# RetNet attention followed by a PReLU feed-forward on one core: the next block's first attention unit enters in the last visit of the block before

## The chip, the cores and the metric

The kernel runs on one core of a Trainium2 chip. The metric is device time in microseconds (us), the median of several executions. In the profile the engines are PE (TensorE, matrix products), PEld (its weight loads), DVE (VectorE), ACT (ScalarE), POOL (GpSimd) and SP (SyncE, which here issues nearly all the DMAs). PSUM is the memory into which the matrix products write; it has eight banks, each of 512 float32 columns on 128 partitions.

## The reference

Two stages follow each other. The first is a retention recurrence per batch and head, with a state of 64 × 64 that decays by a factor of the head; the second is a feed-forward layer over the 3072 tokens, with a leaky ReLU whose slope is learned per hidden column.

```python
batch, n_heads, seq, head_dim = (4, 8, 768, 64)
...
gamma = 1.0 - 2.0 ** (-5.0 - np.arange(H, dtype=np.float32))
scale = 1.0 / np.sqrt(D)
for t in range(S):
    state = gamma[None, :, None, None] * state + np.einsum('bhd,bhe->bhde', k[:, :, t], v[:, :, t])
    y[:, :, t] = scale * np.einsum('bhd,bhde->bhe', q[:, :, t], state)
...
n_tokens, d_model, d_ff = (3072, 512, 2048)
h = x @ w_in
g = np.maximum(h, 0.0) + alpha * np.minimum(h, 0.0)
return (g @ w_out).astype(np.float32)
```

## The kernel before

**Units.** The recurrence is worked in chunks. A unit is 256 positions of one batch and four heads; there are 24 of them, `w` = 0 to 23, two (the head groups) for each stretch of 256 positions. Within a unit the positions form two chunks of 128. Four units (`WB`) make one block of 512 tokens, and there are six blocks, `n` = 0 to 5. Units 4n to 4n + 3 yield the transposed activations `xT[n]` that block n's feed-forward takes.

**What a unit needs.** `load` fetches k, q and v on SP's queue, four units ahead. `prep` scales k and q by their decays on POOL and casts v; from unit 8 on a transposing DMA on SP turns the result into `kq`. `ahead()` does the next unit's `prep` and, behind it, the load of the unit four further on.

**What a unit does on PE, in steps.** All of it is in products on quarters of 64 × 64 of the array.
- `scores(w)` (line 260) multiplies k and q into a pair of PSUM banks with tag `s`; `state_sums(w)` (line 284) multiplies k and v into one or two banks with tag `p`.
- On DVE, `masked(w)` (line 295) turns the scores into the float16 tile `m2`, and so frees `s`; `state(w)` (lines 309 and 311) adds the carried state and decays it, and so frees `p`. A unit with two chunks that both carry on has four such steps.
- `within(w)` (line 344) multiplies the masked scores with v into a pair of banks with tag `y`, then makes the first part of the products with the carried state (line 322). A tiny DVE memset (line 357) behind them tells that they are through.
- `finish(w)` makes the second part of the carried products (line 322 again), which wait for that memset, and ACT copies `y` into `xT` (line 373).

`visit(w_old, w_new)` interleaves two neighbours: `within(w_old)`, `scores(w_new)`, `state_sums(w_new)`, `finish(w_old)`, then `masked(w_new)` and `state(w_new)`. Either may be `None`.

**The feed-forward of a block.** Both halves are generators; `tick(gen, m)` issues the next m matmuls, so that units can be put in between.
- `ffn1(n)` (line 427) makes 16 tiles of 512 hidden columns' worth of output, four matmuls each, 64 in all. For each tile ACT makes `hm` (line 407) and DVE the leaky ReLU (line 396, called a prelu here). Its tiles take their PSUM banks in a written order: `f` is one of two banks `fa` and `fb` in turn, `p` the pair of state banks, and `s`, `S`, `y`, `Y` the first and second halves of the pairs that the units also use.
- `ffn2(n)` (line 444) makes four output tiles of 128 tokens, 16 matmuls of 512 columns each, 64 in all, into `fa` and `fb` in turn. ACT copies each into `os` (line 453), and SP stores it (line 457).

**The order.** The program is scheduled by hand: each engine runs its instructions in the order of the calls, and waits only where data or a buffer asks for it. In the loop for n = 1 to 5, `ffn1(n)` runs with calls of `ahead()` in between, and `ffn2(n)` takes the units of block n + 1 in between: unit w0 = 4(n + 1) enters alone after 2 ticks, three joint visits follow 14 ticks apart, and unit w0 + 3 leaves alone, `within` after 12 more ticks and `finish` 2 ticks later. Six ticks are left. `ahead()` is called at tick 24 and at tick 50. The last block, n = 5, has no units to take in.

Of the kernel before, what the change touches and what calls it, by code (L numbers as in the profile page):

```python
# [9 lines left out]
FP = mybir.dt.float32  # L10
F16 = mybir.dt.float16
COPY = mybir.ActivationFunctionType.Copy
# [6 lines left out]
def kernel(  # L19
# [15 lines left out]
    nc = tc.nc  # L35
    B, H, S, D = q.shape
    d_model, d_ff = moe_w_in.shape
    NFT = d_ff // 128
# [3 lines left out]
    NW = 2 * B * NUS  # L42
    WB = 4
    NBLK = NW // WB
    TB = 512
    scale = 1.0 / np.sqrt(D)
# [31 lines left out]
    sbp = ctx.enter_context(tc.tile_pool(name="sbp", bufs=1, space=bass.MemoryType.SB))  # L78
# [14 lines left out]
    w_out_all = sbp.tile([128, NFT, d_model], F16, tag="wout", name="wout")  # L93
# [5 lines left out]
    def ps(name, tag, n=512, dt=FP, bufs=2):  # L99
        if tag == "f":  # L100
            tag = ("fa", "fb")[flip[0] % 2]
            flip[0] += 1
        if tag in ("fa", "fb"):
            bufs = 1
        return psp.tile([128, n], dt, tag=tag, bufs=bufs, name=name)
# [32 lines left out]
    def place(w):  # L138
        u, g = divmod(w, 2)
        b, c3 = divmod(u, NUS)  # L140
        return u, g, b, c3
# [106 lines left out]
    def half(i):  # L248
        return slice(64 * i, 64 * i + 64)
# [64 lines left out]
    def carried(w, y, started, same, after=None):  # L314
        u, g, b, c3 = place(w)
        kq = live[w][1]
        for x in range(2):
            for r in range(2):
                c = r if same else 1 - r
                if c3 + c == 0:  # L320
                    continue
                ins = nc.tensor.matmul(  # L322
                    out=y[half(x), 256 + 256 * c + 128 * r : 384 + 256 * c + 128 * r],
                    lhsT=tgs[2 * u + c, g][half(r), x, :],
                    rhs=kq[half(r), 4 + 2 * x : 6 + 2 * x, half(c)],
                    start=(c, x) not in started,
                    stop=(same == (c == r)),
                    skip_group_check=True,
                )
                started.add((c, x))  # L330
                if after is not None:
                    behind(ins, after, "the other row half wrote this bank")
                    after = None
        return ins

    def within(w, mid=None, teller=None):
        u, g, b, c3 = place(w)
        vx, m2 = live[w][2:4]
        y = ps("y", "y", 1024, FP, 1)
        started = set()  # L340
        for r in range(2):
            for a in range(2):
                for c, x in DIAG:
                    nc.tensor.matmul(  # L344
                        out=y[half(x), 256 + 256 * c + 128 * r : 384 + 256 * c + 128 * r],
                        lhsT=vx[half(c), 2 * r + x, a, :],
                        rhs=m2[half(c), 2 * r + x, a, :],
                        start=(c, x) not in started,
                        stop=(a == 1 and c3 + c == 0),
                        skip_group_check=True,  # L350
                    )
                    started.add((c, x))
        if mid:
            mid()
        last = carried(w, y, started, True)
        if teller != nc.scalar:
            done = (teller or nc.vector).memset((warm if teller is None else bell)[0:1], 0.0)  # L357
        else:
            done = teller.activation(
                out=word[0:1], in_=word[0:1], func=COPY, bias=0.0, scale=1.0  # L360
            )
        behind(done, last, "tells that the products within the chunks are through")
        live[w].append((y, started, done))

    def finish(w):
        u, g, b, c3 = place(w)
        y, started, done = live[w].pop()
        carried(w, y, started, False, done)
        live.pop(w)
        n, i = divmod(u, 2)  # L370
        if w % WB == 0:
            xT[n] = sbp.tile([128, 2, 4, 2, 128], F16, tag="xT", bufs=2, name=f"xT{n}")
        nc.scalar.activation(  # L373
            out=xT[n][:, g, 2 * i : 2 * i + 2].rearrange("p c r (i a) -> p (c r) i a", a=2),
            in_=y[:, 256:768].rearrange("p (s a i) -> p s i a", a=2, i=64),
            func=COPY,
            bias=0.0,
            scale=1.0,
        )

    def visit(w_old, w_new, cs=None):
        if w_old is not None:
            within(w_old)
        if w_new is not None:
            scores(w_new)
            state_sums(w_new, cs)
        if w_old is not None:
            finish(w_old)
        if w_new is not None:
            masked(w_new)  # L390
            state(w_new, cs)
# [13 lines left out]
    def minus(hps):  # L405
        hm = sbp.tile([128, TB], FP, tag="hm", bufs=3, name="hm")
        nc.scalar.activation(out=hm, in_=hps, func=RELU, bias=0.0, scale=-1.0)  # L407
        return hm

    def ffn1(n, order="spyfSpYf", lead=(0, 0)):  # L410


        gt = sbp.tile([128, NFT, TB], F16, tag="gt", bufs=2, name=f"gt{n}")
        gts[n] = gt
        banks = Banks(order)
        hpss = {}
        narrow, wide = lead
        steps = [(ft, hp, 0, 2) for ft in range(narrow) for hp in range(NP)]
        for hps in ((0, 1), (2, 3)):
            steps += [  # L420
                (ft, hp, 2 if ft < narrow else 0, 4) for ft in range(wide) for hp in hps
            ]
        steps += [(ft, hp, 0, 4) for ft in range(wide, NFT) for hp in range(NP)]
        for ft, hp, lo, hi in steps:
            if hp == 0 and ft not in hpss:
                hpss[ft] = banks.next("hps")
            nc.tensor.matmul(  # L427
                out=hpss[ft][:, 128 * lo : 128 * hi],
                lhsT=w_in_all[:, hp, 128 * ft : 128 * ft + 128],
                rhs=xT[n][:, hp // 2, lo:hi, hp % 2, :],  # L430
                start=(hp == 0),
                stop=(hp == NP - 1),
            )
            if hp == NP - 1 and hi == 4:
                prelu(gt, ft, hpss[ft], 0, TB, minus(hpss.pop(ft)))
            yield

    def ffn2(n, groups=((0,), (1,), (2,), (3,)), tags="ffff"):

        gt = gts.pop(n)  # L440
        for tqs in groups:
            opss = {tq: ps("ops", tags[tq]) for tq in tqs}
            for ft, tq in ((ft, tq) for ft in range(NFT) for tq in tqs):
                nc.tensor.matmul(  # L444
                    out=opss[tq],
                    lhsT=gt[:, ft, 128 * tq : 128 * tq + 128],
                    rhs=w_out_all[:, ft, :],
                    start=(ft == 0),
                    stop=(ft == NFT - 1),
                )  # L450
                if ft == NFT - 1:
                    os_sb = sbp.tile([128, d_model], FP, tag="os", bufs=6, name="os")
                    nc.scalar.activation(  # L453
                        out=os_sb, in_=opss[tq], func=COPY, bias=0.0, scale=1.0
                    )
                    row = TB * n + 128 * tq
                    nc.sync.dma_start(out=out[row : row + 128, :], in_=os_sb)
                yield

    def tick(gen, m):  # L460
        for _ in range(m):
            if next(gen, 1) == 1:
                return
# [9 lines left out]
    for i in range(3):  # L473
# [18 lines left out]
        out=oma_sb, in0=aps[:, 0:NFT], scalar1=-1.0, scalar2=1.0, op0=MULT, op1=ADD  # L492
# [30 lines left out]
    gen = ffn1(0, "ffspypSffYppsfyS", (2, 4))  # L523
# [31 lines left out]
    gen = ffn2(0, ((0, 1), (2,), (3,)), ("fa", "fb", "fa", "fb"))  # L555
# [37 lines left out]
            more[0] += 1  # L593

    for n in range(1, NBLK):
        gen = ffn1(n)
        for i in range(4 if n == 1 else 2):
            tick(gen, 14 if n == 1 else 20)
            ahead()
        for _ in gen:  # L600
            pass
        gen = ffn2(n)
        if n + 1 < NBLK:
            w0 = WB * (n + 1)
            tick(gen, 2)
            visit(None, w0)
            for i in range(1, WB):
                tick(gen, 8)
                if i == 2:
                    ahead()  # L610
                tick(gen, 6)
                visit(w0 + i - 1, w0 + i)
            tick(gen, 6)
            ahead()
            tick(gen, 6)
            within(w0 + WB - 1)
            tick(gen, 2)
            finish(w0 + WB - 1)
        for _ in gen:
            pass  # L620

# [29 lines left out]
```

## Time and profile before

| | us |
|---|---|
| median of 3 executions | 214.1 (213.47 to 215.0) |
| the profiled execution, time | 213.6 |
| the profiled execution, span from first to last instruction | 211.8 |
| mean granted TensorE clock | 0.997 |
| first products (`ffn1`) of blocks 1 to 5 begin at | 53.16, 85.01, 116.82, 148.65, 180.49 |
| second product of block 5 | 194.30 to 208.13 |

The times of rows are microseconds from the span's start; a mean of one instruction is in ns. "x16" counts instructions. In a timeline row the first number is the start and the second the length; square brackets hold the idle time of that engine just before and what ended it. Matmuls overlap in their pipeline, so a matmul row's length is longer than the distance between two starts; the chain of waits gives the distances.

### The profile page before, as it was taken

What the parts mean: (1) busy time and instruction counts of PE and PEld (TensorE: products, weight loads), DVE (VectorE), ACT (ScalarE), POOL (GpSimd) and SP (SyncE); (2) the same over time, 40 slices, a digit from 0 to 9 for tenths busy, and PEclk for the clock granted to TensorE, in tenths of its full rate; (3) what the DMA queues carried; (4) which work ended last, traced back from release to release, by engine and by line L of the source; (5) the groups of instructions that cost most, each with busy time, mean ns of one, the idle gap of its engine ahead of it and who ended that gap; (6) DMA issues with size and microseconds to landing.
All of it is one profiled execution on the core that took longest, in us unless ns stands there. A gap on an engine that the chain in (4) does not pass through costs nothing.

```text
span 211.8 us, 5285 instructions
## 1 busy us (share of the span) xinstructions
PE 205.5 (97%) x2175; PEld 103.8 (49%) x2175; DVE 125.4 (59%) x224; ACT 99.2 (47%) x168; POOL 70.9 (33%) x94
## 2 busy tenths in 40 slices
PE   7999999899999999999999999999999999999992
PEld 8775454364444554444554444554444554444440
DVE  2773986356588733588644588534588733588000
ACT  2685762464765223665223665223665223665121
POOL 0569798349927563544040265000000000000000
PEclk9999999999999999999999999999999999999998
DMA  6999999999999995991364993324500111100111
GB/s 193 348 375 386 304 396 396 300 296 315 321 221 315 274 227 157 263 294 35 88 212 104 218 270 107 89 63 104 147 6 0 50 53 53 50 0 0 53 77 71
DMA packets 63832, 38.28 MB, mean 181 GB/s; under 512 B 19120, under 2 KB 57152, under 8 KB 63808
## 3 DMA queue, kind: packets, MB, share of 16 engines
q1 hardware_dynamic: 63488, 37.76, 62.5%
q8 instruction: 17, 0.28, 0.6%
q10 hardware_dynamic: 320, 0.19, 0.3%
q14 instruction: 7, 0.06, 0.1%
HBM read 27.45 MB, written 6.29 MB: 159 GB/s over the span
## 4 chain that ended last, share of the span: by engine, by line
PE 76%; DMA 13%; POOL 4%; SPq 4%; issue 1%; ACT 0%
PE ops L444 36%; PE hps L427 33%; DMA wo<-in_moe_w_out_dram 6%; SPq L149 4%; PE y L344 3%; DMA wi<-in_moe_w_in_dram 3%; DMA vs<-in_v_dram 3%; PE sc L260 2%; DMA qs<-in_q_dram 2%; POOL win L179 2%; POOL wout L179 1%; PE y L322 1%; PE st L284 1%; POOL kdq L189 1%; ACT os L453 0%
## 5 line engine op out<-in xcount | busy, mean ns | idle before, releaser
L444 PE MATMUL ops<-wout,gt 128*128 128x512 f16 x384 | 89.6, 380 | 0.0
L396 DVE SCALAR_TENSOR_TENSOR gt<-hm,oma,hps 128x512 f16<-128x512 f32 x96 | 71.2, 747 | 28.2 <-ACT hm L407 18.6
L427 PE MATMUL hps<-xT,win 128*128 128x512 f16 (+1 forms) x392 | 84.7, 375 | 0.0
L407 ACT ACTIVATE hm<-hps 128x512 f32<-128x512 f32 x96 | 57.0, 597 | 24.8 <-PE hps L427 24.4
L427 PEld LDWEIGHTS <-win 128*128 128x128 f16 x392 | 37.9, 98 | 44.7 <-issue 0.3
L444 PEld LDWEIGHTS <-gt 128*128 128x128 f16 x384 | 34.9, 98 | 39.8 <-issue 0.5
L189 POOL TENSOR_TENSOR kdq<-ks,tab 128x512 f16<-128x512 f32 x19 | 19.8, 1043 | 42.2 <-DMA ks<-in_k_dram 38.1
L373 ACT ACTIVATE xT<-y 128x512 f16<-128x512 f32 x24 | 14.3, 597 | 40.4 <-PE y L322 40.0
L295 DVE TENSOR_TENSOR m<-sc,mi 128x1024 f16<-128x1024 f32 x24 | 29.3, 1222 | 3.2 <-PE sc L260 1.0
L453 ACT ACTIVATE os<-ops 128x512 f32<-128x512 f32 x24 | 14.2, 597 | 36.1 <-PE ops L444 36.1
L189 POOL TENSOR_TENSOR kdq<-qs,tab 128x512 f16<-128x512 f32 x22 | 23.3, 1058 | 12.0 <-DMA qs<-in_q_dram 12.0
L357 DVE MEMSET warm<- 1x1 f32 x21 | 1.2, 59 | 25.7 <-PE y L322 25.7
L311 DVE TENSOR_TENSOR tg<-st,tab 128x128 f16<-128x128 f32 x40 | 11.6, 289 | 2.0 <-PE st L284 0.9
L322 PE MATMUL y<-kq,tg 64*64 64x128 f16 x160 | 11.5, 228 | 0.0
L179 POOL CAST win<-wi 128x512 f16<-128x512 f32 x16 | 9.8, 613 | 3.3 <-DMA wi<-in_moe_w_in_dram 2.9
L309 DVE TENSOR_TENSOR st<-tg,st 128x128 f32<-128x128 f16 x32 | 9.3, 291 | 2.5 <-PE st L284 0.6
L344 PEld LDWEIGHTS <-vx 64*64 64x64 f16 x384 | 6.4, 106 | 8.6 <-issue 6.6
L260 PE MATMUL sc<-kq 64*64 64x128 f16 x384 | 10.0, 218 | 0.5 <-ACT kq L238 0.3
L238 ACT ACTIVATE kq<-trb 128x512 f16<-128x512 f16 (+1 forms) x12 | 8.6, 735 | 3.5 <-PE trb L232 3.4
L344 PE MATMUL y<-m,vx 64*64 64x128 f16 x384 | 10.0, 221 | 0.1
L179 POOL CAST wout<-wo 128x512 f16<-128x512 f32 x16 | 9.6, 613 | 1.4 <-DMA wo<-in_moe_w_out_dram 1.1
L209 POOL CAST vx<-vs 128x512 f16<-128x512 f32 x16 | 9.8, 610 | 0.5 <-PE ops L444 0.2
(26 smaller groups left out, 66.1 us busy)
## 6 DMA issues: line engine op xcount, KB each, us to landing
ks<-in_k_dram SPq DMA_DIRECT2D x24, 256.0 KB, 4.2
qs<-in_q_dram SPq DMA_DIRECT2D x24, 256.0 KB, 4.6
vs<-in_v_dram SPq DMA_DIRECT2D x24, 256.0 KB, 4.6
out_dram<-os SPq DMA_DIRECT2D x24, 256.0 KB, 2.5
wi<-in_moe_w_in_dram SPq DMA_DIRECT2D x16, 256.0 KB, 5.4
wo<-in_moe_w_out_dram SPq DMA_DIRECT2D x16, 256.0 KB, 5.7
kq<-kdq SPq DMA_TRANSPOSE x16, 4.2
mi<-mi_const ACTq DMA_DIRECT2D x1, 128.0 KB, 2.9
```

Of the source, the lines that this page charges most:

```text
L179: nc.gpsimd.tensor_copy(out=dst, in_=t)
L189: eng.tensor_tensor(out=kdq[:, kind].rearrange("p z r d -> p r z d"), in0=src.rearrange("p (r x) (a d) -> p r (x a) d", a=2, x=2), in1=tab ...
L260: nc.tensor.matmul(out=sc[half(c), at : at + 128], lhsT=kq[half(r), 2 * x + a, half(c)], rhs=kq[half(r), 4 + 2 * x : 6 + 2 * x, half(c)], ...
L295: nc.vector.tensor_tensor(out=m2.rearrange("p s a i -> p s (a i)"), in0=sc.rearrange("p (s n) -> p s n", n=256), in1=mask.unsqueeze(1).to_ ...
L322: ins = nc.tensor.matmul(out=y[half(x), 256 + 256 * c + 128 * r : 384 + 256 * c + 128 * r], lhsT=tgs[2 * u + c, g][half(r), x, :], rhs=kq[ ...
L344: nc.tensor.matmul(out=y[half(x), 256 + 256 * c + 128 * r : 384 + 256 * c + 128 * r], lhsT=vx[half(c), 2 * r + x, a, :], rhs=m2[half(c), 2 ...
L373: nc.scalar.activation(out=xT[n][:, g, 2 * i : 2 * i + 2].rearrange("p c r (i a) -> p (c r) i a", a=2), in_=y[:, 256:768].rearrange("p (s ...
L396: nc.vector.scalar_tensor_tensor(out=gt[:, ft, lo:hi], in0=hm, scalar=oma_sb[:, ft : ft + 1], in1=hps, op0=MULT, op1=ADD,)
L407: nc.scalar.activation(out=hm, in_=hps, func=RELU, bias=0.0, scale=-1.0)
L427: nc.tensor.matmul(out=hpss[ft][:, 128 * lo : 128 * hi], lhsT=w_in_all[:, hp, 128 * ft : 128 * ft + 128], rhs=xT[n][:, hp // 2, lo:hi, hp ...
L444: nc.tensor.matmul(out=opss[tq], lhsT=gt[:, ft, 128 * tq : 128 * tq + 128], rhs=w_out_all[:, ft, :], start=(ft == 0), stop=(ft == NFT - 1),)
L453: nc.scalar.activation(out=os_sb, in_=opss[tq], func=COPY, bias=0.0, scale=1.0)
```

## The change

From block 2 on, `ffn2` no longer begins with a unit entering alone. Instead the last unit of a block leaves in a joint visit in which the first unit of the next block enters: at the end of block 1 unit 12, of block 2 unit 16, of block 3 unit 20. Unit 8 still enters alone in block 1, and unit 23 leaves in block 4 in a visit without a partner, its `finish` straight behind its `within`. The first joint visit of blocks 2 to 4 comes after 16 ticks, as before, and the calls of `ahead()` stay at ticks 24 and 50; the last visit comes at tick 57.

From block 2 on `ffn1` takes its banks in another order. In block 5 the last output tile is made in two halves of 256 columns, each with its own bank, 16 matmuls, copy and store; the copy of the second half is shared between ACT and DVE, 128 columns each.

```diff
-    def ffn2(n, groups=((0,), (1,), (2,), (3,)), tags="ffff"):
+    def ffn2(n, groups=((0,), (1,), (2,), (3,)), tags="ffff", split=()):
         gt = gts.pop(n)
         for tqs in groups:
-            opss = {tq: ps("ops", tags[tq]) for tq in tqs}
...
+            parts = [slice(0, 512)]
+            if tqs[0] in split:
+                parts = [slice(0, 256), slice(256, 512)]
+            for at in parts:
+                m = at.stop - at.start
+                opss = {tq: ps("ops", tags[tq])[:, 0:m] for tq in tqs}
+                for ft, tq in ((ft, tq) for ft in range(NFT) for tq in tqs):
+                    nc.tensor.matmul(
+                        out=opss[tq],
+                        lhsT=gt[:, ft, 128 * tq : 128 * tq + 128],
+                        rhs=w_out_all[:, ft, at],
...
+                    if ft == NFT - 1:
+                        os_sb = sbp.tile([128, d_model], FP, tag="os", bufs=6, name="os")[:, 0:m]
+                        cut = 128 if at.start else m
+                        nc.scalar.activation(
+                            out=os_sb[:, 0:cut],
+                            in_=opss[tq][:, 0:cut],
...
+                        if cut < m:
+                            nc.vector.tensor_copy(out=os_sb[:, cut:m], in_=opss[tq][:, cut:m])
+                        row = TB * n + 128 * tq
+                        nc.sync.dma_start(out=out[row : row + 128, at], in_=os_sb)
+                    yield
...
     for n in range(1, NBLK):
-        gen = ffn1(n)
+        gen = ffn1(n, "fspyfSpY" if n > 1 else "spyfSpYf")
...
-        gen = ffn2(n)
-        if n + 1 < NBLK:
-            w0 = WB * (n + 1)
+        gen = ffn2(n, split=(3,) if n + 1 == NBLK else ())
+        w0 = WB * (n + 1)
+        if n == 1:
             tick(gen, 2)
             visit(None, w0)
+        if n + 1 < NBLK:
             for i in range(1, WB):
-                tick(gen, 8)
+                tick(gen, 10 if n > 1 and i == 1 else 8)
                 if i == 2:
                     ahead()
                 tick(gen, 6)
                 visit(w0 + i - 1, w0 + i)
             tick(gen, 6)
             ahead()
-            tick(gen, 6)
-            within(w0 + WB - 1)
-            tick(gen, 2)
-            finish(w0 + WB - 1)
+            tick(gen, 7)
+            visit(w0 + WB - 1, w0 + WB if w0 + WB < NW else None)
         for _ in gen:
             pass
```

More of the change, by code (lines that the diff above doesn't have):

```diff
@@ L436, in ffn1 @@
             yield
-    def ffn2(n, groups=((0,), (1,), (2,), (3,)), tags="ffff"):
+    def ffn2(n, groups=((0,), (1,), (2,), (3,)), tags="ffff", split=()):
         gt = gts.pop(n)
         for tqs in groups:
-            opss = {tq: ps("ops", tags[tq]) for tq in tqs}
[L443 to L454, printed above, removed]
-                    )
-                    row = TB * n + 128 * tq
-                    nc.sync.dma_start(out=out[row : row + 128, :], in_=os_sb)
-                yield
+            parts = [slice(0, 512)]
[9 more added lines that the diff above has]
+                        rhs=w_out_all[:, ft, at],
+                        start=(ft == 0),
+                        stop=(ft == NFT - 1),
+                    )
+                    if ft == NFT - 1:
[4 more added lines that the diff above has]
+                            in_=opss[tq][:, 0:cut],
+                            func=COPY,
+                            bias=0.0,
+                            scale=1.0,
+                        )
+                        if cut < m:
[3 more added lines that the diff above has]
+                    yield
```

## The prediction

> **What bounds the kernel now.** I read the page's busy times first.
>
> ```profile
> PE 205.5 (97%) x2175; PEld 103.8 (49%) x2175; DVE 125.4 (59%) x224; ACT 99.2 (47%) x168; POOL 70.9 (33%) x94
> ```
>
> TensorE (PE) is busy 97% of the span, no other engine over 59%. What matters is whether PE stands still between blocks, so next I cut the span at the block boundaries; this is block 1's second product (stretch: us, then per engine busy time and count, granted clock, DMA share, GB/s).
>
> ```profile
> 66.97:85.01 18.04, 18.04 (x274) 8.94 (x272) 9.49 (x22) 4.70 (x8) 9.02 (x11) 1.00 0.98 227
> ```
>
> PE is busy for all of its 18.04 us, at granted clock 1.00. Its pieces stand in the chain of waits in order of time (start, us, what):
>
> ```profile
> 66.97 0.43 PE ops L444 x2
> 67.40 0.35 PE sc L260 x16
> 67.75 0.12 PE st L284 x16
> 67.88 3.13 PE ops L444 x14
> 71.00 0.35 PE y L344 x16
> 71.35 0.06 PE y L322 x4
> 71.41 0.22 PE sc L260 x16
> 71.63 0.12 PE st L284 x16
> 71.75 0.09 PE y L322 x4
> 71.85 3.13 PE ops L444 x14
> ...
> 82.48 0.35 PE y L344 x16
> 82.83 0.06 PE y L322 x4
> 82.89 0.54 PE ops L444 x2
> 83.43 0.18 PE y L322 x4
> 83.61 1.40 PE ops L444 x6
> 85.01 13.81 PE hps L427 x64
> ```
>
> The last row is the next first product: 64 matmuls of 512 columns in 13.81 us, 0.2158 each. The second product has 64 such matmuls too, so the attention units between them cost 18.04 − 13.81 = 4.23 us, and the change rearranges only those.
>
> Fourteen ops matmuls at 0.2158 are 3.02 us, but each run of fourteen takes 3.13: the first big matmul after small 64-row tiles pays 0.11. Small after big pays too: scores cost 0.35 behind ops and 0.22 behind other small products. So every entry and exit costs about 0.11, and fewer interruptions are cheaper with the same products.
>
> - A unit entering alone: 0.35 + 0.12 + 0.11 = 0.58.
> - A joint visit: 0.85 (71.00 to 71.85) + 0.11 = 0.96.
> - The last unit leaving alone, in two pieces: 0.35 + 0.06, then 0.54 − 0.43 = 0.11, then 0.18, then 1.40 − 6 × 0.2158 = 0.105; together 0.805.
>
> Check: 0.58 + 3 × 0.96 + 0.805 = 4.27 against 4.23 measured.
>
> **The change, block by block.** At the ends of blocks 1, 2 and 3 the last unit leaves in a joint visit with unit 12, 16 or 20 (0.96 in place of 0.805), and blocks 2, 3 and 4 no longer open with a unit entering alone (0.58 gone).
>
> Block 1: +0.155. Blocks 2 and 3: 0.155 − 0.58 = −0.425 each. Block 4 loses its entry, and its last unit, 23, leaves with nobody entering and without the two ticks that stood between `within` and `finish`. There the second products wait for the telling memset:
>
> ```profile
> 107.28 0.06 DVE L357 MEMSET warm<- 1x1 f32 x1 [1.60 <-PE y L322]
> 107.39 0.10 PEld L322 LDWEIGHTS <-tg 64*64 64x64 f16 x2
> 178.15 0.23 PE L322 MATMUL y<-kq,tg 64*64 64x128 f16 x4
> 178.30 0.60 PE L444 MATMUL ops<-wout,gt 128*128 128x512 f16 x2
> 178.44 0.06 DVE L357 MEMSET warm<- 1x1 f32 x1 [1.58 <-PE y L322]
> ```
>
> The memset ends at 178.50 and weights follow one 0.05 later (107.34 to 107.39), so PE stands from 178.30 to 178.55, 0.25 us. It saves the exchange: second products at 0.09 and not 0.18, no 0.11 in between. New cost 0.40 + 0.25 + 0.09 + 0.105 = 0.845, +0.04. Block 4: −0.54. The first term is 0.155 − 0.425 − 0.425 − 0.54 = **−1.24 us**.
>
> **What hides the moved work.** No DMA and no POOL work moves: `ahead()` still stands at ticks 24 and 50 of the second product, so SP's stores, transposes and loads keep their order. What moves is 16 scores, 8 or 16 state products, one mask and up to four state steps on DVE, from after the next first product to before it. Call T the end of the joint visit on PE. A present visit shows what follows (its ops begin at T = 107.56):
>
> ```profile
> 107.48 1.23 DVE L295 TENSOR_TENSOR m<-sc,mi 128x1024 f16<-128x1024 f32 x1
> 107.56 3.20 PE L444 MATMUL ops<-wout,gt 128*128 128x512 f16 x14
> 107.71 0.60 ACT L373 ACTIVATE xT<-y 128x512 f16<-128x512 f32 x1 [3.36 <-PE y L322]
> 109.67 0.29 DVE L311 TENSOR_TENSOR tg<-st,tab 128x128 f16<-128x128 f32 x1
> 117.72 0.60 ACT L407 ACTIVATE hm<-hps 128x512 f32<-128x512 f32 x1 [0.27 <-PE hps L427]
> 118.36 10.24 DVE L396 SCALAR_TENSOR_TENSOR gt<-hm,oma,hps 128x512 f16<-128x512 f32 x12 [3.52 <-ACT hm L407]
> ```
>
> The mask is through at T + 1.15, the state steps at T + 2.4, the xT copy at T + 0.75. Seven ticks (0.11 + 7 × 0.2158 = 1.62) lie between T and the next first product, so the xT copy has 0.87 to spare. The new order `fspyfSpY` asks for `s` only at its second tile, T + 2.48, and for `p` at T + 3.3: free 1.3 and 0.9 earlier. DVE idled 3.52 us before its first prelu, at 118.36. That prelu can start once the first tile's four matmuls (0.86), a wait of 0.27 and ACT's 0.60 are past, so near T + 1.62 + 1.75 = T + 3.4: the state steps end 1.0 earlier. I cost this queue move at nothing; without this cover the 2.4 us of DVE would stand before PE.
>
> The entering unit's kq must have landed. Its transposes, SP's queue, and the spread of their landings:
>
> ```profile
> 72.13 2.62 SPq L202 DMA_TRANSPOSE kq<-kdq  x1
> 81.88 1.30 SPq L202 DMA_TRANSPOSE kq<-kdq  x1
> DMA to landing us min/median/max: 2.7/4.2/6.4
> ```
>
> The row at 72.13 is unit 12's, the one at 81.88 unit 13's. With the longest landing, counted even from the issue's end, unit 12 is there at 72.13 + 2.62 + 6.4 = 81.15. The joint visit begins one tick after 82.48 and its scores 0.41 later, at 83.1: 2 us spare at worst, 6.8 at the median from the issue's start.
>
> **The tail.**
>
> ```profile
> 16.34 0.61 PE L427 MATMUL hps<-xT,win 128*128 128x256 f16 x4
> L427 PE MATMUL hps<-xT,win 128*128 128x256 f16 x16 | 2.6, 275 | 0.0
> 208.15 0.60 ACT L453 ACTIVATE os<-ops 128x512 f32<-128x512 f32 x1 [2.86 <-PE ops L444]
> 208.77 0.33 SPq L457 DMA_DIRECT2D out_dram<-os  x1
> L238 ACT ACTIVATE kq<-trb 128x1024 f16<-128x1024 f16 x4 | 4.1, 1022 | 1.8 <-PE trb L232 1.8
> L309 DVE TENSOR_TENSOR st<-tg,st 128x128 f32<-128x128 f16 x32 | 9.3, 291 | 2.5 <-PE st L284 0.6 <-DVE tg L311 0.5
> GB/s 0 0 0 0 0 0 117 410 433 410 129 0 0 0 0 0 0 0 0 0 0 0 0 0 0 0 246 386 421 386 59 0 0 0 0 0 0 0 0 0
> ```
>
> Matmuls: four of 256 columns take 0.61 with 0.275 for the last, so they start (0.61 − 0.275) / 3 = 0.112 apart. 32 of them take 3.58, against 16 × 0.2158 = 3.45: **+0.13**.
>
> Copies: ACT takes 0.60 for the 512 columns and 1.022 for 1024, so a column costs 0.83 ns and 128 columns 0.60 − 384 × 0.00083 = 0.28; the f16 form is the only one of another width. DVE's 128 columns are a new form; 0.291 (two inputs) is the nearest row, a lower end is the 0.06 memset, and I take 0.25. Side by side they take 0.28 in place of 0.60, −0.32. One behind the other: ACT hands to DVE in 0.04 (ACT's 0.60 from 117.72 against DVE at 118.36, above), so 0.28 + 0.04 + 0.25 = 0.57, −0.03. Nothing in this trace shows two engines reading one bank side by side, and they read columns of one bank here, so I take **−0.03** and keep −0.32 as the far end. [...]
>
> Store: the last GB/s row covers 205 to 212 us in 0.175 us slices; the last 256 KB move at about 410 GB/s once flowing, 0.64 us. The first half now leaves 1.8 us earlier, so 128 KB remain: **−0.32**, between 0 (if rows of half the length move at half the rate) and −0.64. [...]
>
> **Sum.** −1.24 + 0.13 − 0.03 − 0.32 = −1.46 us. The profiled execution took 213.6 (span 211.8 and 1.8 around it), so 212.1; it lay 0.5 under the median of 214.1, and on that median the forecast is **212.6 us**, −0.7%. A difference under 1% (2.1 us) is about what a measurement of this kernel cannot tell from no change, and that is the forecast's class.
>
> **Rivals.**
>
> *Copies side by side.* For it: they touch different columns. Against: one bank, and no example. −1.46 − 0.29 = −1.75, 212.3.
>
> *Given back at the boundary.* The prelus of the next first product start late because DVE still holds the entering unit, or a bank of the new order is late. For it: the spares are only 0.9 to 1.3 us. Against: PE has no gap now, and ACT and DVE idle there. If each of three boundaries loses the 0.4 it gained, only the tail and part of block 4 remain, about −0.3: 213.8.
>
> *The entering unit's kq is late: slower.* Place: the scores of units 12, 16 and 20. It decides once a transpose lands after 83.1 (and its like in blocks 2 and 3). If the transpose were held behind two stores as unit 13's is at 81.88, it would land at 81.88 + 4.2 = 86.1, and PE would stand 3 us three times: +9.0 − 1.5, 221.6. Against: unit 12's transpose is called at tick 24, ahead of the second store.
>
> *The change does nothing.* Only if the joint visits were empty; the loop's arguments name units 12, 16 and 20, so I give it no chance apart from the giving back.
>
> **Chances.** Forecast 0.52, side by side 0.22, given back 0.15, late kq 0.06, something unseen 0.05, half of it slower. Faster by over 1% needs −2.14: a sixth of the forecast, a third of the second case with run-to-run spread (213.47 to 215.0): 0.09 + 0.07 and a little of the unseen, 0.18. Slower by over 1%: 0.06 + 0.02 = 0.08. Within: 0.74. The forecast with its bounds (store 0 to −0.64, copies, about 0.4 us of spread) spans 211.5 to 213.5; taking in the given-back case, the range is 211.2 to 214.2, leaving out late kq, the unseen and the fringe.
>
> **What would show it.** Right: the second products of blocks 2 and 3 take 17.65 us, of block 1 18.2, of block 4 17.5; PE busy throughout; the last matmul to the end of the span 0.35 shorter. Wrong: a PE gap before `sc` (late kq) or within the first four tiles of a first product (a bank or DVE); DVE's copy beginning with ACT's and not behind it; the last 32 matmuls wider apart than 0.112.

## The result, and the profile after

Over 20 executions of each kernel the median went from 214.9 to 213.41 us. The ratio is 0.9934, with a 95% interval of 0.9907 to 0.996: 0.7% faster, clear of no change and inside the 1% within which the forecast had put it. A ratio leaves out executions more than 1.5% above the fastest of their kernel, here 3 of the changed kernel's 20, and so can differ a little from that of the medians. The forecast of 212.6 was counted from a median of three executions, 214.1; over 20 the kernel before took 214.9, and so the time came out 0.8 above the forecast although the difference fits. The profiled execution took 213.21 us with a span of 211.4, only 0.4 less than the span before, although the median fell by 1.5. The chain of waits in order of time shows where the rest is. These rows (start, us, what) are the end of block 1 and the start of block 2 in the changed kernel:

```profile
83.63 0.35 PE y L344 x16
83.98 0.06 PE y L322 x4
84.04 0.22 PE sc L260 x16
84.26 0.12 PE st L284 x16
84.38 0.09 PE y L322 x4
84.48 1.62 PE ops L450 x7
86.09 13.81 PE hps L427 x64
99.91 3.45 PE ops L450 x16
103.36 0.35 PE y L344 x16
```

The joint visit stands in one piece, the next first product follows without a gap, and block 2's second product opens with 16 matmuls in 3.45 us, with nothing entering alone. The first row of block 1 (`54.09 13.81 PE hps L427 x64` in the same view) begins 0.93 us later than before: the head of the program, which the change does not touch, was slower in this execution. From there on everything can be compared. From first product to first product, before and after, and then to the end of the span:

| | before | after | difference | predicted |
|---|---|---|---|---|
| block 1 | 31.85 | 32.00 | +0.15 | +0.155 |
| block 2 | 31.81 | 31.39 | −0.42 | −0.425 |
| block 3 | 31.83 | 31.38 | −0.45 | −0.425 |
| block 4 | 31.84 | 31.42 | −0.42 | −0.54 |
| block 5 to the end of the span | 31.31 | 31.12 | −0.19 | −0.22 |
| sum, from block 1 to the end | 158.64 | 157.31 | −1.33 | −1.46 |

The fall of the median, 1.5, lies nearer to the predicted 1.46 than the 1.33 of the table, but by its interval it is anything from 0.9 to 2.0, so that is chance; the table is the better measure.

The end, in the timeline of the changed kernel (start, length, engine, line, instruction, idle time before it):

```profile
207.98 0.28 ACT L460 ACTIVATE os<-ops 128x128 f32<-128x128 f32 x1 [1.36 <-PE ops L450]
208.29 0.29 DVE L468 COPY os<-ops 128x128 f32<-128x128 f32 x1 [12.78 <-ACT os L460]
208.61 0.33 SPq L470 DMA_DIRECT2D out_dram<-os  x1
```

DVE's copy begins 0.03 after ACT's ends and names ACT as what it waited for: the two read the same bank one behind the other, and together they take 0.60, as ACT's single copy of 512 columns did.

### The profile page after: what moved, and what is told of

The parts are those of the page before. It is cut to its first block, busy times and chain, and to the rows that moved or that the text cites. A ratio compares the mean times of both kernels' runs of the same rounds, so it can differ in the third digit from the quotient of the medians.

```text
span 211.4 us, 5322 instructions
## 1 busy us (share of the span) xinstructions
PE 204.2 (97%) x2191; PEld 105.7 (50%) x2191; DVE 125.8 (59%) x225; ACT 99.2 (47%) x169; POOL 71.2 (34%) x94
## 4 chain that ended last, share of the span: by engine, by line
PE 76%; DMA 13%; POOL 4%; SPq 4%; issue 1%; DVE 0%; ACT 0%
PE ops L450 36%; PE hps L427 33%; SPq L149 4%; DMA ks<-in_k_dram 3%; PE y L344 3%; DMA vs<-in_v_dram 3%; DMA wi<-in_moe_w_in_dram 3%; DMA wo<-in_moe_w_out_dram 2%; POOL wout L179 2%; DMA qs<-in_q_dram 2%; PE sc L260 2%; POOL kdq L189 2%; PE y L322 1%; PE st L284 1%; POOL win L179 1%
## 5 line engine op out<-in xcount | busy, mean ns | idle before, releaser
L450 PE MATMUL ops<-wout,gt 128*128 128x512 f16 (+1 forms) x400 | 88.2, 371 | 0.0
L427 PE MATMUL hps<-xT,win 128*128 128x512 f16 (+1 forms) x392 | 84.7, 375 | 0.0
L427 PEld LDWEIGHTS <-win 128*128 128x128 f16 x392 | 38.0, 98 | 44.7 <-issue 0.3
L450 PEld LDWEIGHTS <-gt 128*128 128x128 f16 x400 | 37.1, 98 | 39.4
L460 ACT ACTIVATE os<-ops 128x512 f32<-128x512 f32 (+2 forms) x25 | 14.3, 576 | 34.5 <-PE ops L450 34.5
```

The costliest lines, as they stand in the source:

```text
L427: nc.tensor.matmul(out=hpss[ft][:, 128 * lo : 128 * hi], lhsT=w_in_all[:, hp, 128 * ft : 128 * ft + 128], rhs=xT[n][:, hp // 2, lo:hi, hp ...
L450: nc.tensor.matmul(out=opss[tq], lhsT=gt[:, ft, 128 * tq : 128 * tq + 128], rhs=w_out_all[:, ft, at], start=(ft == 0), stop=(ft == NFT - 1),)
L460: nc.scalar.activation(out=os_sb[:, 0:cut], in_=opss[tq][:, 0:cut], func=COPY, bias=0.0, scale=1.0,)
```

## Experiments

Each kernel is compared with the kernel before on the same chip. As the head of the program alone moved by up to 4.4 us between executions (the last section), each is also read by the stretch from the first product of block 1 to the end of the span, in its own profile: 158.64 before, 157.31 for the whole change. A span is given to 0.1, so a difference of two such stretches holds to about 0.1; the blocks, read from the chain of waits, hold to 0.01.

**1. The joint visits alone.**

```diff
-        gen = ffn2(n, split=(3,) if n + 1 == NBLK else ())
+        gen = ffn2(n, split=())
```

> The joint visits and the bank order alone; the last output tile stays in one piece. Theory (fewer exchanges between big and small products): block 1 takes 32.0 us from first product to first product, blocks 2 to 4 31.4, as in the profile of the whole change, against 31.85 in the kernel before; together -1.15 us, ratio 0.9945. Rival (the gain is in the tail): ratio 0.999 to 1.001.

Ratio 0.9931 (0.9894 to 0.9969). The blocks took 32.0, 31.4, 31.39 and 31.42, and the stretch from block 1 on 211.6 − 54.03 = 157.57, 1.07 less than before. The joint visits carry the change.

**2. The split of the last tile alone**, in the loop of the kernel before.

```diff
-        gen = ffn2(n)
+        gen = ffn2(n, split=(3,) if n + 1 == NBLK else ())
```

> The last output tile in two halves alone, with the loop of the kernel before. Theory: blocks as before (31.85 us each), the last product and the tail 0.2 us shorter, ratio 0.999. Rival (the gain is in the tail): ratio about 0.994.

The blocks were 31.85, 31.82, 31.81 and 31.85, as before, and the stretch from block 1 on 215.8 − 57.28 = 158.52, 0.12 less. But the ratio was 1.0034 (1.0003 to 1.0065), on the wrong side. Block 1 began at 57.28 in that profile, 4.1 later than in the one before. So it was run again.

> The split of the last tile alone once more, since its ratio of 1.0034 went against a profile in which everything from block 1 on took 0.1 us less than before. Theory (the head of the program, up to block 1, differs by up to 4 us from execution to execution and that is what the ratio caught): from the first product of block 1 to the end 158.5 us again, and a ratio whose interval holds 1. Rival (the split costs time in a way the stretch from block 1 on does not show): a ratio of 1.003 again, with its interval above 1.

The second time the stretch took 213.2 − 54.72 = 158.48 and the ratio was 1.0008 (0.9976 to 1.004). The interval holds 1: by the two profiles the split gains 0.12 and 0.16 us, little more than their rounding, and no ratio of this size can see that. That the first ratio's excess was the head of the program fits both profiles; the executions behind a ratio were not all profiled, so it is not shown for each.

**3. ACT copies the whole second half.**

```diff
-                        cut = 128 if at.start else m
+                        cut = m
```

> The whole change, but ACT copies all 256 columns of the second half and DVE none. Theory (the two copies run one behind the other, 0.28 + 0.02 + 0.29): one copy of 256 columns takes 0.38 like the first half's, so the end comes 0.2 us sooner than in the whole change: from the last matmul to the end of the span 3.2 us in place of 3.44, ratio to the kernel before 0.9925. Rival (the second engine helps): the end comes later by 0.1.

The end of the chain of waits in this kernel:

```profile
195.36 13.87 PE ops L450 x80
209.23 0.02 issue
209.25 0.38 ACT os L460
```

One copy of 256 columns takes 0.38, against 0.60 for two copies of 128 on two engines. From block 5's first product to the end it took 30.95, where the whole change took 31.12; from block 1 on 212.5 − 55.34 = 157.16. Ratio 0.9947 (0.9918 to 0.9975). By the profile the sharing of the copy costs 0.17 us.

**4. The old order of the banks.**

```diff
-        gen = ffn1(n, "fspyfSpY" if n > 1 else "spyfSpYf")
+        gen = ffn1(n)
```

> The whole change with the bank order of before (spyfSpYf) in every block. Theory (seven big matmuls and nothing else stand between the joint visit and the first tile, 1.62 us, and the mask frees the score banks after 1.15): no gap on PE, blocks 2 to 4 still 31.4 us, ratio as for the whole change, 0.9934. Rival (the order is needed): PE stands ahead of the first tile of blocks 2 to 4, up to 1.2 us each, ratio up to 1.01.

Blocks 2 to 4 took 31.39, 31.38 and 31.42, to a hundredth those of the whole change; from block 1 on 214.9 − 57.55 = 157.35. Ratio 0.9907 (0.9869 to 0.9945). The new order of banks buys no time here. The ratio lies below the whole change's 0.9934, but the intervals overlap, and no block shows a gain.

**5. One tick in the exit without a partner**, with experiment 3's edit.

```diff
-            visit(w0 + WB - 1, w0 + WB if w0 + WB < NW else None)
+            if w0 + WB < NW:
+                visit(w0 + WB - 1, w0 + WB)
+            else:
+                within(w0 + WB - 1)
+                tick(gen, 1)
+                finish(w0 + WB - 1)
```

> The whole change with ACT copying the whole second half, and with one tick between within and finish of unit 23, the exit without a partner. Theory (the wait for the telling memset, 0.25 us, is covered by one big matmul, and the second products then cost 0.18 in place of 0.25): block 4 takes 31.28 us from first product to first product in place of 31.42; with the copy, 0.3 us less from the first product of block 1 to the end than the whole change, 157.0 in place of 157.3. Rival (the exchange to the big matmul and back costs as much as the wait): block 4 stays at 31.42.

The chain of waits at that exit, first in the whole change, then with the tick:

```profile
177.82 0.35 PE y L344 x16
178.17 0.09 PE y L322 x2
178.26 0.04 issue
178.30 0.07 DVE warm L357
178.37 0.04 issue
178.41 0.25 PE y L322 x4
178.66 1.62 PE ops L450 x7
```

```profile
178.55 0.35 PE y L344 x16
178.90 0.06 PE y L322 x4
178.95 0.32 PE ops L450
179.27 0.18 PE y L322 x4
179.45 1.40 PE ops L450 x6
```

In the first the chain leaves PE for the memset and comes back, and the second products cost 0.25 behind a PE that stood still. In the second the chain stays on PE: one big matmul covers the memset. Block 4 took 31.26 in place of 31.42. From block 1 on: 211.8 − 54.8 = 157.0, 1.64 less than before. The ratio was 0.9862 (0.9817 to 0.9907), more than 1.64 us can explain (0.9923), so this kernel was compared again.

> The version with one tick in the last exit and ACT's copy once more, beside the split alone on the same chip. Theory: 157.0 us from the first product of block 1 to the end again, 1.64 less than before, ratio 0.9923, so that the 0.9862 of its first comparison was in part the head of the program. Rival (the extra gain is real): 0.986 again.

Again 211.8 − 54.88 = 156.92 from block 1 on, and a ratio of 0.9947 (0.991 to 0.9983). The two intervals do not overlap, while the two profiles agree within 0.1 us; 0.9923 lies in the second one. What lies ahead of block 1 is the only part that differs between the two profiled executions by more than that, but the executions behind the first ratio were not profiled one by one, so its excess stays unexplained. This is the best version: 0.3 to 0.4 us under the whole change by the profile, which no ratio here resolves.

**6. Two big matmuls inside the last visit.**

```diff
-    def visit(w_old, w_new, cs=None):
+    def visit(w_old, w_new, cs=None, gap=None):
         if w_old is not None:
             within(w_old)
+        if gap:
+            tick(gap, 2)
...
-            tick(gen, 7)
-            visit(w0 + WB - 1, w0 + WB if w0 + WB < NW else None)
+            tick(gen, 5)
+            visit(w0 + WB - 1, w0 + WB if w0 + WB < NW else None, None, gen)
```

> The whole change, but in the last visit of blocks 1 to 4 two of the big matmuls stand between within and what follows, and two fewer ahead of the visit. Theory (each exchange between big and small products costs about 0.11 to 0.13 us of PE): blocks 1 to 3 take 0.24 longer each (32.24, 31.63, 31.63) with the same instructions; block 4 0.1 to 0.15 shorter, as its wait is covered. Rival (what a unit costs is its own products, wherever they stand): no block changes.

The same stretch of the chain of waits as in the result's first fence, now with the two matmuls in between:

```profile
84.18 0.35 PE y L344 x16
84.52 0.06 PE y L322 x4
84.58 0.54 PE ops L452 x2
85.12 0.35 PE sc L260 x16
85.47 0.12 PE st L284 x16
85.59 0.06 PE y L322 x4
85.65 1.62 PE ops L452 x7
```

The kernel ran once, in 214.64 us, and is read by its profile alone. Two matmuls that cost 0.43 elsewhere cost 0.54 here, and the same 16 scores 0.35 in place of 0.22. Blocks 1 to 3 took 32.2, 31.59 and 31.6, so 0.2 longer each with the same instructions, and block 4 31.27, 0.15 shorter, its wait being covered. So here the cost of a unit depended on how often PE went between the two kinds of products.

**7. Nothing behind the last visit.**

```diff
-            tick(gen, 7)
+            tick(gen, 14)
```

> The whole change with the last visit of blocks 1 to 4 at the very end of the second product, all 64 of its matmuls ahead of it, so that nothing stands between the visit and the next first product. Theory (the seven matmuls hide the copy of y into xT, through 0.75 after the visit, and the mask, through after 1.15; the first tile goes to f and waits for xT alone): PE stands about 0.7 us in each of the four blocks, 32.7, 32.1, 32.1 and 32.1. Rival (the state steps on DVE, 2.4 us after the visit, are what the next block waits for): 1.5 us or more each.

The chain of waits at the end of block 1:

```profile
88.31 0.15 PE y L322 x4
88.46 0.02 issue
88.48 0.60 ACT xT L373
89.08 0.04 issue
89.13 13.54 PE hps L427 x62
102.67 1.51 PE ops L450 x7
```

This kernel too ran once, in 216.98 us. It is the copy into xT that PE waits for, as the theory said, not DVE. But the second products now begin at 70.32, 102.67, 134.38, 166.12 and 197.86, 32.35, 31.71, 31.74 and 31.74 apart, where the whole change has 32.00, 31.38, 31.39 and 31.41: 0.33 to 0.35 a block, half of the 0.7 expected. The row of 62 says why. A unit fills the half of xT of its head group; the first two matmuls of a tile read the other half, which the unit before filled, and they ran ahead of the wait (2 × 0.2158 = 0.43, which leaves 0.27 of the 0.7). Of the rest, the second products take 0.15 in place of 0.09. The rival's 1.5 us did not come.

**8. The entering unit prepared late.**

```diff
-                if i == 2:
+                if i == 2 and n > 3:
                     ahead()
...
             tick(gen, 6)
+            if n <= 3:
+                ahead()
             ahead()
```

> The whole change, but in blocks 1 to 3 the preparation of the entering unit is called at tick 50 with its neighbour's, behind the third store on SP's queue, in place of tick 24. Theory (the joint visit is free only because unit 12, 16 or 20 has its kq in time): its transpose goes out near 82 on the scale of the profile before, lands 4.2 us later, and PE stands about 3 us ahead of the scores in blocks 1, 2 and 3, together about 9 us, ratio 1.035. Rival (the transposes have slack enough): no gap, ratio 0.9934.

The chain of waits in block 2, then the clock around that stall (stretch: us, busy times and counts of PE, PEld, DVE, ACT and POOL, granted clock, DMA share, GB/s):

```profile
117.51 4.54 DMA kq<-kdq
122.05 0.04 issue
122.10 0.64 PE sc L260 x16
...
123.06 3.10 PE ops L450 x7
126.16 0.85 PE hps L427 x2
```

```profile
118.50:122.00 3.50, 0.27 (x20) 0.10 (x8) 0.06 (x1) 0.00 (x0) 0.00 (x0) 0.89 0.69 166
122.00:127.50 5.50, 5.40 (x39) 2.43 (x40) 1.72 (x3) 1.19 (x2) 3.29 (x4) 0.50 1.01 279
```

The transpose goes out behind the third store and PE stands until it lands. In the profiled execution, which took 226.88 us, blocks 1 to 3 took 33.67, 36.73 and 36.37, so 1.7, 5.3 and 5.0 more than in the whole change, 12.0 together. PE stood for 1.51, 3.33 and 2.19 of them, 7.0 and not the theory's 9. The other 5 came with the clock: in block 2 PE ran at granted clock 0.50 from 122.00 to 127.50, so that seven big matmuls took 3.10 in place of 1.62, and behind block 3's stall the clock was 0.55 in the mean from 158.70 to 162.50. The second execution took 222.32, against a median of 215.52 before: a ratio of 1.032, near the theory's 1.035. It has no profile of its own, but its mean granted clock was 0.989 and the first one's 0.974. By an estimate from these means and the spans, the first lost (1 − 0.974) × 225.1 = 5.9 us of clock and the second (1 − 0.989) × 220.5 = 2.4; the 3.5 between these are most of the 4.6 between the two times. So a total near 9 does not show three stalls of 3.

## Why the prediction held

**The exchange between big and small products** was the right mechanism, and its sizes were right: the joint visit in place of two interruptions is worth 0.42 to 0.45 a block (blocks 2 and 3), and block 1 pays 0.15 for its longer last visit. Experiment 1 has the gain without the split, and experiment 6 takes half of one block's gain away by two matmuls put in the wrong place. One of the signs was worked out wrongly: 18.04 − 0.425 is 17.62 and not 17.65 for the second products of blocks 2 and 3; block 2's took 17.57 (99.91 to 117.48), 0.43 less than before (98.82 to 116.82, 18.00).

**Block 4's exit was mis-sized.** "It saves the exchange: second products at 0.09 and not 0.18, no 0.11 in between. New cost 0.40 + 0.25 + 0.09 + 0.105 = 0.845, +0.04." Up to the start of the second products at 178.41 the exit took 0.59 (0.35 + 0.09 and 0.15 of standing still), where 0.40 + 0.25 had been foreseen. But behind an idle PE the second products cost 0.25 and not 0.09. With the 0.11 of the exchange behind it the exit costs 0.95: +0.15 against before, and not +0.04.

**The cover was right.** Apart from the memset in block 4's exit, PE waits for nothing at the four boundaries of the changed kernel. DVE in its timeline at the tightest, where unit 20 enters with four state steps:

```profile
149.28 0.29 DVE L311 TENSOR_TENSOR tg<-st,tab 128x128 f16<-128x128 f32 x1
150.40 1.61 DVE L396 SCALAR_TENSOR_TENSOR gt<-hm,oma,hps 128x512 f16<-128x512 f32 x2 [0.82 <-ACT hm L407]
```

It still idles 0.82 before its first prelu; 1.0 had been worked out. So the giving back at the boundary did not happen. Of its parts the copy into xT is the one with a price when the seven matmuls go (experiment 7), and the banks have room even in their old order (experiment 4).

**The late kq** did not happen either; experiment 8 shows that the rival was real, and that it sets in when the transpose stands behind the third store. Its price of 9 had the wrong parts: PE stands for 7.0, and what the clock adds behind the stalls, 5 in the profiled execution, was not foreseen.

**The tail** was right in sum, −0.19 against −0.22, by three terms that were each a little off. The last product, as the chain of waits groups it, and the landings of the stores after 204 us:

```profile
194.09 13.87 PE ops L450 x80
```

```profile
out_dram<-os SPq DMA_DIRECT2D x1, 256.0 KB, 2.0
out_dram<-os SPq DMA_DIRECT2D x2, 128.0 KB, 1.7
```

The 32 narrow matmuls added 0.04 (13.87 against 13.83) and not 0.13: they start (13.87 − 48 × 0.2158) / 32 = 0.110 apart, and not 0.112. The copies take the 0.60 that one took, so their 0.03 did not come. The store of 128 KB lands in 1.7 in place of 2.0, and from its issue to the end of the span it is 211.4 − 208.61 = 2.79 in place of 3.03: −0.24 against −0.32. So from the last matmul to the end of the span it was 3.44 in place of 3.67, 0.23 shorter and not the 0.35 that was named as a sign. By the landings, given to 0.1, the half store is 0.3 shorter; the end came 0.24 sooner.

**The copies** ran one behind the other, as taken, in the time of one. DVE's copy waited for ACT's, 0.28 and then 0.29, and no run here lets them overlap. The rival of copies side by side falls; experiment 3 shows that sharing the copy is 0.2 slower than not sharing it.

## What to carry to other kernels

In this kernel PE has no gap, and what was left to gain, 0.42 to 0.45 us a block, was in how often it goes between kinds of products. In a kernel like it, read the cost of an exchange from the first row behind it (3.13 for what is 14 × 0.2158 = 3.02 in the first product), count the interruptions, and put neighbours together, with enough other work behind them to hide the copy that the next stage waits for (without it a block took 0.33 to 0.35 more, experiment 7). The exit that waited for another engine took 0.16 less with one piece of work in between than with none (31.26 against 31.42, experiment 5). Before sharing one PSUM bank's evacuation between two engines, look whether the second starts before the first ends: here it began 0.03 after, and the sharing cost 0.17 (experiment 3).

## What the runs showed of the hardware

**The head of the program varies more than the change is worth.** Up to block 1 the same instructions took from 53.16 (the kernel before) to 57.55 us (experiment 4), and one kernel took 57.28 and 54.72 in its two profiles (experiment 2). The difference is there early, in what the DMA engines deliver. The stretch from 5 to 20 us of the kernel before, and of experiment 4 (last column GB/s):

```profile
5.00:20.00 15.00, 14.37 (x306) 10.70 (x305) 9.09 (x18) 9.50 (x19) 10.22 (x15) 1.00 1.10 367
```

```profile
5.00:20.00 15.00, 11.77 (x286) 8.95 (x284) 8.94 (x17) 8.36 (x17) 7.04 (x9) 1.00 0.97 288
```

With 367 GB/s block 1 began at 53.16, with 288 at 57.55. Three others had 333 GB/s with block 1 at 54.09 (the whole change), 307 with 54.88 (the second profile of experiment 5's kernel) and 271 with 57.28 (the first of experiment 2's; the mean of 291, 284 and 238 over three stretches of 5 us). Mostly the lower the rate is, the later block 1 begins. No run sets the rate, so that it is the cause is not shown, and why it differs was not found. From block 1 on, two executions of one kernel agree within 0.1 us in the two cases at hand (158.52 and 158.48; 157.0 and 156.92), so that a stretch of the profile ranks versions that whole-kernel ratios cannot.

**Behind stalls of 2.19 and 3.33 us PE's granted clock was about half.** In experiment 8 it was 0.50 behind a stall of 3.33 in block 2 (122.00 to 127.50, above), 0.55 in the mean behind one of 2.19 in block 3, and 1.00 behind one of 1.51 in block 1. The stretches behind the stalls of blocks 1 and 3, and between them the one in which block 2's clock comes back:

```profile
87.00:89.40 2.40, 2.19 (x44) 1.26 (x45) 1.61 (x3) 0.60 (x1) 0.49 (x1) 1.00 0.86 238
127.50:131.00 3.50, 3.50 (x16) 1.53 (x15) 2.06 (x3) 2.13 (x4) 1.94 (x3) 0.92 0.77 213
158.70:162.50 3.80, 3.79 (x42) 1.87 (x43) 2.31 (x5) 0.60 (x1) 0.00 (x0) 0.55 0.13 29
```

In block 2 the clock was lower already within the stall, 0.89 in the mean over 118.50 to 122.00 (above). The length of a stall need not be what decides: in the first profile of experiment 2 the clock was 0.78 from 15 to 20 us and 0.88 from 20 to 25, where PE was busy for 4.01 and 5.00 of the 5 us. What makes the clock fall, and how long it stays down, no run here shows.
